# Half of w_out converted in the last part, in two passes over the tokens, with a new order of the attention

## The chip, the cores and the metric

The kernel runs on one core of one Trainium2 chip. What counts is the device time of one execution in microseconds; of several runs the median is taken. The engines have short names: PE multiplies matrices (PEld is its loading of weights), DVE, ACT and POOL work on elements, SP issues most of the transfers (DMA). Each engine works through its own instructions in the order in which they were written, and waits on semaphores for the others. The granted clock of PE is in the profile's rows; 1.00 stands for 2.4 GHz.

## What is computed

Three stages follow each other. First an attention for 4 batches of 8 heads, in which the 1152 queries are averaged in pairs, to 576. Its output, as 2304 tokens of 512 numbers, goes through a soft mixture of 8 experts with 4 slots each. The result goes through a feed-forward layer of width 2048 with `h * cos(h)`:

```python
q_pool = q.reshape(B, H, S // factor, factor, D).mean(axis=3)
scores = scale * np.matmul(q_pool, k.transpose(0, 1, 3, 2))
scores = scores - np.max(scores, axis=-1, keepdims=True)
attn = np.exp(scores)
attn = attn / (np.sum(attn, axis=-1, keepdims=True) + 1e-09)
out = np.matmul(attn, v)
...
logits = x @ phi
d = softmax over tokens; slot_input = d.T @ x
slot_out[e] = np.maximum(slot_input[e] @ w1[e], 0.0) @ w2[e]
x = softmax over slots(logits) @ slot_out
...
h = x @ w_in
g = h * np.cos(h)
y = (g @ w_out).astype(np.float32)
```

Heads are worked on in 16 pairs `p`; the 288 queries of one half `a` of a pair make a half-pair, 32 in all, each with 9 tiles `t` of 128 keys. That gives 288 score tiles.

## The kernel before

**Attention.** For one score tile PE makes the scores of two heads (L460, with the negated maximum added at L463), ACT the exponentials (E, L471), PE the product with V (L498). The row sums of the exponentials (ES, L486 and L488) are added by DVE or by POOL; the table `VEC` names for each half-pair the tiles that DVE adds. The maxima come from an extra product (L415) that DVE reduces (L424). PSUM has four places of two banks for all these; an operation that takes one waits until the last reader of the one before is done. The table `ORDER` lists 2500 operations in the order in which they are written to the engines' queues; nothing else decides it.

**Conversions in the attention.** The weights w_in and w_out are 64-bit numbers; each of 32 tiles of 128 x 512 is turned into 32-bit ones and written to DRAM (`w32`): a load `raw` (512 KB), two ACT steps (L289, L294), three DVE steps (L298, L304, L310), an addition on POOL (L316), a store of 256 KB. Tiles 0 to 15 are w_in, 16 to 31 w_out. There is one buffer `raw` and one `cvt`, so the tiles follow each other, about one per nine score tiles.

**The experts** run from about 500 to 541 us, with their weights streaming in, and end with the slot outputs `soT` (L1280).

**The last part.** `make_p`, `make_p1` and `put_p` multiply `soT` with w_in into `Pst`, which has four tiles of 512 columns. Then the 9 blocks of 256 tokens are worked on in units; a unit is a block and two (at the start one) of the 16 tiles `f` of 128 hidden columns. Per unit PE makes `u` (L1397), ACT and DVE make `g` (L1402 to L1413), DVE splits off a rounded part `hi` (L1415), POOL the rest `lo` (L1417), and PE adds 12 products to two sums `o0` and `o1` (L1433, L1435), each in one of two buffers. For that each tile of w_out is split into `w_hi` and `w_lo` as well (`split_w`, L1317 to L1321; the table `SPLIT` gives the engines). After a block's last unit ACT empties both sums into `ob` (L1445) and SP stores them. `START` lists the first steps by hand (`s` a split, `p` a part of Pst, `u`, `g` and `o` a unit's three steps); after that a loop writes, for unit `no`, `u` of unit no + 4, `g` of unit no + 2 and `o` of unit no, in this order. Before, there are 9 units in the first block and 8 in each of the other eight, 73 in all.

## Time and profile before

| | |
|---|---|
| median of 3 runs | 773.59 us (773.06 to 776.13) |
| the profiled execution | 778.18 us |
| its span in the profile | 776.4 us |
| PE, DVE, ACT, POOL busy in the span | 737.1, 587.7, 448.9, 409.5 us |
| moved by DMA | 101.48 MB, 131 GB/s on average |

The profiled execution took 4.59 us more than the median of the runs, and 1.78 us of it lie around the span. Sums are made against its own time. PE's records overlap, since one matmul is fed in while the one before drains; so "busy" says when PE had something in flight, and a dense run is read from the distance of the starts. Idle time is told with what ended it, the releaser.

### The profile page before, as it was taken

The page shows a single profiled execution, that of the slowest core. Times are in us where ns is not written, and L with a number is a line of the kernel's source. Part 1 is how long each engine was busy: PE and PEld are TensorE (multiplying, and loading weights), DVE is VectorE, ACT ScalarE, POOL GpSimd, SP SyncE. Part 2 cuts the span into 40 slices and gives each one's busy share as a digit, 9 for nine tenths or more (in the row PEclk, how much of TensorE's full clock was granted, in tenths as well). Part 3 has the DMA queues.
Part 4 walks back from the last instruction along what each step waited for, and adds up shares of the span by engine and source line. Part 5 has one row for each costly group of instructions (what it writes and reads, how often), then busy time and mean ns, then how long its engine had stood idle before and what let it go on. Part 6 is the DMA issues. An engine that isn't in the chain of part 4 may idle for free.

```text
span 776.4 us, 16372 instructions
## 1 busy us (share of the span) xinstructions
PE 737.1 (95%) x6336; PEld 532.1 (69%) x6336; DVE 587.7 (76%) x935; ACT 448.9 (58%) x838; POOL 409.5 (53%) x340
## 2 busy tenths in 40 slices
PE   5999999999899999999989998899999999999997
PEld 3766667676676676677666766433678888888886
DVE  6899999988888889899889897322686656565652
ACT  2556656576565666566566653223767666656661
POOL 1476666775669574856456630013765444444442
PEclk9999999999999999999999999999999999999999
DMA  8444465366654654646153456599801010000101
GB/s 201 111 122 142 116 194 143 100 164 174 198 144 137 199 137 140 185 138 162 52 157 103 140 164 211 190 365 385 302 1 28 27 29 28 10 17 28 29 28 27
DMA packets 86482, 101.48 MB, mean 131 GB/s; under 512 B 48260, under 2 KB 48260, under 8 KB 86404
## 3 DMA queue, kind: packets, MB, share of 16 engines
q1 hardware_dynamic: 80384, 100.09, 43.1%
q10 hardware_dynamic: 6020, 0.34, 0.6%
q8 instruction: 50, 0.82, 0.4%
q14 instruction: 28, 0.23, 0.1%
HBM read 87.10 MB, written 13.11 MB: 129 GB/s over the span
## 4 chain that ended last, share of the span: by engine, by line
PE 48%; DVE 9%; ACT 2%; issue 2%; POOL 1%; ACTq 0%; DVEq 0%; POOLq 0%
PE o L1433 16%; PE o L1435 8%; PE mx L498 6%; PE mx L460 4%; DVE nm L424 2%; PE po L1262 2%; PE u L1397 2%; PE h L1229 2%; PE mx L415 2%; DVE ES L488 1%; PE mx L463 1%; PE pm L1341 1%; POOL ES L488 1%; ACT E L471 1%; PE mx L442 0%
## 5 line engine op out<-in xcount | busy, mean ns | idle before, releaser
L488 POOL TENSOR_TENSOR ES<-ES,E 128x576 f32<-128x576 f32 x142 | 208.2, 1467 | 94.5 <-DVE ES L488 66.6
L424 DVE TENSOR_REDUCE nm<-mx 128x2 f32<-128x768 f32 x240 | 221.3, 950 | 26.7 <-PE mx L415 25.8
L471 ACT ACTIVATE E<-mx 128x576 f32<-128x576 f32 x288 | 177.4, 651 | 83.3 <-PE mx L463 62.6
L460 PE MATMUL mx<-Q,kX 64*128 64x288 f32 x1152 | 171.5, 314 | 9.9 <-DVE nm L424 4.7
L498 PE MATMUL mx<-E,vn 128*64 128x288 f32 x1152 | 157.7, 414 | 3.0 <-DVE nm L424 2.2
L1417 POOL TENSOR_TENSOR lo<-g,hi 128x512 fp32r<-128x512 f32 (+1 forms) x73 | 94.3, 1291 | 110.4 <-DVE hi L1415 106.1
L460 PEld LDWEIGHTS mx<-Q,kX 64*128 64x128 f32 x1152 | 111.8, 190 | 30.3 <-DVE nm L424 11.5
L498 PEld LDWEIGHTS mx<-E,vn 128*64 128x64 f32 x1152 | 75.8, 137 | 59.1 <-ACT E L471 8.0
L1433 PE MATMUL o<-w_hi,hi 128*128 128x512 f32 x288 | 113.1, 393 | 0.7 <-DVE hi L1415 0.7
L1435 PE MATMUL o<-w_lo,hi 128*128 128x512 f32 x288 | 113.2, 393 | 0.3 <-DVE w_lo L1321 0.3
L415 PE MATMUL mx<-kX,Q 64*128 64x384 f32 x480 | 87.6, 387 | 5.7 <-DVE nm L424 4.7
L460 PE MATMUL mx<-Q,kY 64*128 64x288 f32 x576 | 87.2, 297 | 0.0
L463 PE MATMUL mx<-NM,one_row 64*128 64x288 f32 x576 | 86.9, 296 | 0.0
L1433 PE MATMUL o<-w_hi,lo 128*128 128x512 f32 x288 | 77.4, 389 | 0.0
L1404 DVE SCALAR_TENSOR_TENSOR r<-t,u 128x512 f32<-128x512 f32 (+1 forms) x73 | 49.4, 679 | 36.4 <-ACT t L1402 35.8
L1402 ACT ACTIVATE t<-u 128x512 f32<-128x512 f32 (+1 forms) x73 | 43.0, 591 | 58.0 <-PE u L1397 57.9
L1413 DVE SCALAR_TENSOR_TENSOR g<-r,u 128x512 f32<-128x512 f32 (+1 forms) x73 | 49.6, 679 | 35.5 <-ACT r L1411 34.8
L316 POOL TENSOR_TENSOR cvt<-cvt 128x512 uint32<-128x512 uint32 x32 | 43.4, 1357 | 61.9 <-DVE cvt L310 28.7
L415 PEld LDWEIGHTS mx<-kX,Q 64*128 64x128 f32 x480 | 44.9, 190 | 28.6 <-DVE nm L424 10.9
L488 DVE TENSOR_TENSOR ES<-ES,E 128x576 f32<-128x576 f32 x81 | 61.5, 759 | 2.8 <-POOL ES L488 0.5
L1433 PEld LDWEIGHTS o<-w_hi,lo 128*128 128x128 f32 x288 | 54.1, 188 | 11.5
L1433 PEld LDWEIGHTS o<-w_hi,hi 128*128 128x128 f32 x288 | 54.2, 188 | 10.8 <-DVE hi L1415 0.9
(227 smaller groups left out, 1016.2 us busy)
## 6 DMA issues: line engine op xcount, KB each, us to landing
w<-in_moe_w_dram SPq DMA_DIRECT2D x85, 256.0 KB
...
```

The costliest lines, as they stand in the source:

```text
L415: nc.tensor.matmul(out=m[:, h, 0:384], lhsT=Q1[p % 2][hs, AT[i]:AT[i] + 128], rhs=X[p][hs, ks], start=True, stop=True)
L424: nc.vector.tensor_reduce(out=nm3[p][:, i, :, c:c + 1], in_=m[:, :, 0:384], axis=AX.X, op=ALU.max)
L460: nc.tensor.matmul(out=sc[:, h, 0:HF], lhsT=x[hs, ks], rhs=y[hs, qs], start=(n == 0), stop=False)
L463: nc.tensor.matmul(out=sc[:, h, 0:HF], lhsT=one_row[hs, :], rhs=NM[p % 2][hs, qs], start=False, stop=True)
L471: nc.scalar.activation(out=e, in_=sc[:, :, 0:HF], func=AF.Exp, scale=1.0 / 16.0)
L488: eng.tensor_tensor(out=ES[p, a], in0=ES[p, a], in1=E[p, a, t], op=ALU.add)
L498: nc.tensor.matmul(out=av_t[p, a, g][64 * h:64 * h + 64, 0:HF], lhsT=vn[p][:, h, t, :], rhs=E[p, a, t][:, h, :], start=(t == g), stop=(t = ...
L1404: nc.vector.scalar_tensor_tensor(out=r, in0=t, scalar=MAGIC, in1=u, op0=ALU.subtract, op1=ALU.subtract)
L1413: nc.vector.scalar_tensor_tensor(out=g, in0=r, scalar=1.0, in1=u, op0=ALU.subtract, op1=ALU.mult)
L1417: nc.gpsimd.tensor_tensor(out=lo[:, 0:n], in0=g, in1=hi[:, 0:n].bitcast(FP32), op=ALU.subtract)
L1433: nc.tensor.matmul(out=o, lhsT=x, rhs=w_hi[ff], start=(ff == 0 and not part), stop=bool(part and ff == NF - 1))
L1435: nc.tensor.matmul(out=o, lhsT=x, rhs=w_lo[ff], start=False, stop=False)
```

## The change

`NU` falls from 32 to 24: tiles 24 to 31, the second half of w_out, are no longer converted in the attention. `ORDER` has 2436 operations, in a new order throughout, and `VEC` is new. The last part goes over the tokens twice. In the first pass (units 0 to 36) the first eight tiles `f` are used, and each block's sums are stored to DRAM (`part_o`); in the second pass (units 37 to 72) the other eight, and DVE adds the sums that are loaded back (`kept`). The eight conversions run in the first pass, as `THEN` says: for each tile a load four units ahead (for the first in unit 5), ACT's steps in unit t, DVE's first two in t + 1, sign and POOL's addition in t + 2, the split in t + 4, with t = 7, 11, ... 35. The tile isn't written to DRAM and read back; the split takes it from `cvt`. `raw` and `cvt` take over the buffers of `win1`. Two rounds of `put_p` move from `START` to units 9 and 11.

```diff
 GAHEAD = 2
-FIRST = (1, 1, 2, 2, 2, 2, 2, 2, 2)
-SPLIT = (0, 1, 1, 3, 1, 1, 1, 3, 2, 0, 1, 0, 3, 3, 0, 1)
+FIRST = (1, 1, 2, 2, 2)
+SPLIT = (0, 1, 1, 3, 1, 1, 1, 3, 1, 1, 1, 1, 1, 1, 1, 1)
...
     ("g", 0), ("s", 3), ("g", 1), ("p", 1, 0, 512), ("u", 2), ("o", 0), ("s", 5), ("s", 6), ("s", 4), ("u", 3),
-    ("g", 2), ("u", 4), ("o", 1), ("g", 3), ("p",), ("g", 4), ("s", 7), ("o", 2), ("p", 2), ("s", 11), ("u", 5),
-    ("u", 6), ("s", 9), ("s", 10), ("p", 3), ("s", 14), ("g", 5), ("o", 3), ("s", 8), ("s", 15), ("o", 4),
-    ("g", 6), ("s", 13), ("s", 12), ("u", 7), ("g", 7), ("u", 8), ("u", 9), ("o", 5), ("g", 8), ("u", 10),
-    ("g", 9), ("o", 6), ("u", 11), ("g", 10), ("o", 7), ("o", 8), ("o", 9),
+    ("g", 2), ("u", 4), ("o", 1), ("g", 3), ("s", 7), ("p",), ("u", 5), ("g", 4), ("o", 2), ("u", 6), ("g", 5), ("u", 7),
+    ("o", 3), ("g", 6), ("u", 8), ("g", 7), ("o", 4), ("u", 9),
 )
+def then():
+    do = {9: [("p", 2)], 11: [("p", 3)]}
+    for f in range(8, 16):
+        t = 4 * (f - 8) + 7
+        for step, at in enumerate((max(t - 4, 5), t, t + 1, t + 2, t + 4)):
+            do.setdefault(at, []).append(("c", f, step))
+    return do
+THEN = then()
...
 VEC = (
-    "468", "1", "45", "2468", "25", "237", "4", "1267",
-    "36", "6", "6", "12367", "68", "67", "15", "7",
-    "568", "1", "4578", "126", "4", "24568", "4", "2367",
-    "234", "17", "238", "137", "67", "123568", "2345678", "1234567",
+    "58", "12", "7", "125", "128", "14", "25", "13568",
+    "23", "68", "123", "7", "56", "56", "48", "1346",
+    "168", "12", "4567", "26", "125", "28", "478", "2",
+    "348", "1", "127", "6", "678", "368", "2345678", "1234567",
 )
 ORDER = (
-    "020304050709060G080H0A0OXsXt0PXu0Q0R0M0N0E0F0C0D0S0I0J0K0L2429010T2A0U0X0Y0V0b0W0m23250B2C0n0p0t0x0qXvXwXxXyXz26"
...
+    "0v470X0i0Y27282BXx0o0s0-X+000Z100f0g0w0z0a0+12130dXy0e14150b0c1819111C1D0j4A161G1H1A1E2W2Q2X171B0k0l1FXz2RX-1J1K"
...
     NU_I = HP * DFF // 512
-    NU = NU_I + NF
+    NU = NU_I + NF // 2
     w32 = [dr.tile([128, 512], FP32, name=f"w32_{i}") for i in range(NU)]
     cv = {}
+    cv_p = [lambda shape, tag: per.tile(shape, U32, tag=tag, name=tag)]
     def conv_load(i):
-        if i >= NU:
-            return
         if i < NU_I:
...
             src = w_out[(i - NU_I) * 128:(i - NU_I + 1) * 128, :]
-        raw = per.tile([128, 512, 2], U32, tag="raw", name="raw")
+        raw = cv_p[0]([128, 512, 2], "raw")
         nc.sync.dma_start(out=raw.rearrange("p a b -> p (a b)"), in_=src)
...
         raw = cv[i]
-        t = per.tile([128, 2, 512], U32, tag="cvt", name="cvt")
+        t = cv_p[0]([128, 2, 512], "cvt")
         t, r = t[:, 0], t[:, 1]
...
         TB = 256
+        NA = NF // 2
+        cv_p[0] = lambda shape, tag: wo.tile(shape, U32, tag="win1_0" if tag == "raw" else "win1_1", name=tag)
+        part_o = [dr.tile([128, DM], FP32, name=f"po{i}") for i in range(NTOK // 128)]
         Pst = [op.tile([128, 512], F32R, bufs=1, name=f"Pst{f}") for f in range(DFF // 512)]
-        win1 = [wo.tile([128, 2, 512], FP32, name=f"win1_{kk}") for kk in range(HP)]
+        win1 = [wo.tile([128, 2, 512], FP32, tag=f"win1_{kk}", name="win1") for kk in range(HP)]
         spread = op.tile([128, 4, 192], F32R, bufs=1, name="spread")
...
+        def late_w(f, step):
+            i = NU_I + f
+            if step == 0:
+                conv_load(i)
+            elif step == 1:
+                conv_act(i)
+                conv_low(i)
+            elif step == 2:
+                conv_clamp(i)
+                conv_shift(i)
+            elif step == 3:
+                conv_sign(i)
+                conv_round(i)
+            else:
+                w_lo[f] = wo.tile([128, DM], F32R, tag=f"w_lo{f}", name="w_lo")
+                split_w(f, cv.pop(i).bitcast(FP32))
         def load_w(f):
...
-        def split_w(f):
+        def split_w(f, w=None):
+            w = w_lo[f].bitcast(FP32) if w is None else w
             if SPLIT[f] // 2:
-                nc.vector.tensor_copy(out=w_hi[f], in_=w_lo[f].bitcast(FP32))
+                nc.vector.tensor_copy(out=w_hi[f], in_=w)
             else:
-                nc.scalar.activation(out=w_hi[f], in_=w_lo[f].bitcast(FP32), func=AF.Copy)
+                nc.scalar.activation(out=w_hi[f], in_=w, func=AF.Copy)
             eng = nc.gpsimd if SPLIT[f] % 2 else nc.vector
-            eng.tensor_tensor(
-                out=w_lo[f], in0=w_lo[f].bitcast(FP32), in1=w_hi[f].bitcast(FP32), op=ALU.subtract
-            )
+            eng.tensor_tensor(out=w_lo[f], in0=w, in1=w_hi[f].bitcast(FP32), op=ALU.subtract)
...
         units = []
-        for blk in range(NTOK // TB):
-            f0 = 0
-            for n in FIRST if blk == 0 else (UF,) * (NF // UF):
-                units.append((blk, f0, n))
-                f0 += n
+        for half in range(2):
+            for blk in range(NTOK // TB):
+                f0 = half * NA
+                for n in FIRST if blk == 0 and half == 0 else (UF,) * (NA // UF):
+                    units.append((blk, f0, n))
+                    f0 += n
         us, gs = {}, {}
...
-        acc = {}
+        acc, kept = {}, {}
...
             last = i == len(units) - 1
+            second = f0 >= NA
+            first_f, last_f = (NA, NF - 1) if second else (0, NA - 1)
+            if second and f0 == NA:
+                kept[blk] = wo.tile([128, 2, DM], FP32, tag=f"win1_{2 + blk % 2}", name="kept")
+                for s in range(2):
+                    nc.sync.dma_start(out=kept[blk][:, s], in_=part_o[2 * blk + s])
...
                 ff = f0 + f
-                if ff == 0 and part == 0:
+                if ff == first_f and part == 0:
                     acc[blk, s] = ps_o.tile([128, DM], FP32, tag=f"o{s}", name=f"o{s}")
...
                 x = (lo if part else hi)[:, f, s * 128:(s + 1) * 128]
-                nc.tensor.matmul(out=o, lhsT=x, rhs=w_hi[ff], start=(ff == 0 and not part), stop=bool(part and ff == NF - 1))
+                nc.tensor.matmul(out=o, lhsT=x, rhs=w_hi[ff], start=(ff == first_f and not part), stop=bool(part and ff == last_f))
                 if not part:
...
                 ob = op.tile([128, DM], FP32, tag="ob", name="ob")
-                if last:
-                    h = DM // 2
-                    nc.scalar.activation(out=ob[:, 0:h], in_=o[:, 0:h], func=AF.Copy, scale=-TWOPI)
-                    nc.vector.tensor_scalar(out=ob[:, h:], in0=o[:, h:], scalar1=-TWOPI, scalar2=None, op0=ALU.mult)
-                else:
+                if not second:
                     nc.scalar.activation(out=ob, in_=o, func=AF.Copy, scale=-TWOPI)
+                    nc.sync.dma_start(out=part_o[2 * blk + s], in_=ob)
+                    return
+                nc.vector.scalar_tensor_tensor(out=ob, in0=o, scalar=-TWOPI, in1=kept[blk][:, s], op0=ALU.mult, op1=ALU.add)
...
                     store(x[0])
-            if f0 + n == NF and not last:
+            if f0 + n == last_f + 1 and not last:
                 for s in range(2):
...
                 make_p(*a, pm)
-                if a[2] == 512:
-                    for i in range(4):
-                        load_w(NF - 8 + 4 * a[0] + i)
...
                 ng += 1
+            for f, *args in THEN.get(no, ()):
+                {"p": more_p, "c": late_w}[f](*args)
             emit_o(no)
...
```

The tables alone don't show what moves. Three places follow, with line numbers of before and after, each as the engine's instructions stand there in a row.

DVE late in the attention, around the maxima of the last pair of heads (nm), before:

```order
L513 TENSOR_TENSOR avs<-mx,avs 128x288
L424 TENSOR_REDUCE nm_6630<-mx 128x2
L298 TENSOR_SCALAR cvt<-cvt 128x512
L304 TENSOR_SCALAR cvt<-cvt 128x512
L486 TENSOR_TENSOR ES<-E 128x576
L488 TENSOR_TENSOR ES<-ES,E 128x576 x2
L310 SCALAR_TENSOR_TENSOR cvt<-raw,cvt 128x512
L424 TENSOR_REDUCE nm_6630<-mx 128x2 x3
L488 TENSOR_TENSOR ES<-ES,E 128x576 x2
```

and after:

```order
L519 TENSOR_TENSOR avs<-mx,avs 128x288
L430 TENSOR_REDUCE nm_6591<-mx 128x2
L494 TENSOR_TENSOR ES<-ES,E 128x576
L430 TENSOR_REDUCE nm_6591<-mx 128x2 x2
L494 TENSOR_TENSOR ES<-ES,E 128x576
L430 TENSOR_REDUCE nm_6591<-mx 128x2 x3
L494 TENSOR_TENSOR ES<-ES,E 128x576
L430 TENSOR_REDUCE nm_6591<-mx 128x2
L595 TENSOR_TENSOR xT<-avs,mx 128x576
```

The three conversion steps (cvt) are gone, and the sums (ES) stand singly between the maxima.

DVE at the start of the last part, from the cast of `w_hi` of tile 7 on, before:

```order
L1317 CAST w_hi_7937<-w_lo 128x512
L1321 TENSOR_TENSOR w_lo<-w_lo,w_hi_7941 128x512
L1404 SCALAR_TENSOR_TENSOR r<-t,u 128x512 x2
L1321 TENSOR_TENSOR w_lo<-w_lo,w_hi_7939 128x512
L1372 CAST Pst_7915<-pm 128x512
L1321 TENSOR_TENSOR w_lo<-w_lo,w_hi_7944 128x512
L1413 SCALAR_TENSOR_TENSOR g<-r,u 128x512
L1415 CAST hi<-g 128x512
L1317 CAST w_hi_7938<-w_lo 128x512
L1321 TENSOR_TENSOR w_lo<-w_lo,w_hi_7938 128x512
```

and after:

```order
L1345 CAST w_hi_7867<-w_lo 128x512
L1387 SCALAR_TENSOR_TENSOR p_lo<-pm,p_hi 128x256
L1431 SCALAR_TENSOR_TENSOR r<-t,u 128x512
L1440 SCALAR_TENSOR_TENSOR g<-r,u 128x512
L1442 CAST hi<-g 128x512
L1431 SCALAR_TENSOR_TENSOR r<-t,u 128x512
L1440 SCALAR_TENSOR_TENSOR g<-r,u 128x512
L1442 CAST hi<-g 128x512
L1431 SCALAR_TENSOR_TENSOR r<-t,u 128x512
L1440 SCALAR_TENSOR_TENSOR g<-r,u 128x512
```

The splits of the later tiles and the copy of Pst (L1372) are gone from between the steps of the units; r, g and hi follow each other.

POOL at the end of the first pass; w_hi_7874 and w_hi_7875 are tiles 14 and 15. Before, behind the splits of the start, it had nothing but `lo` (L1417 x66). After:

```order
L322 TENSOR_TENSOR cvt<-cvt 128x512
L1444 TENSOR_TENSOR lo<-g,hi 128x512 x2
L1349 TENSOR_TENSOR w_lo<-cvt,w_hi_7874 128x512
L1444 TENSOR_TENSOR lo<-g,hi 128x512 x2
L322 TENSOR_TENSOR cvt<-cvt 128x512
L1444 TENSOR_TENSOR lo<-g,hi 128x512 x2
L1349 TENSOR_TENSOR w_lo<-cvt,w_hi_7875 128x512
L1444 TENSOR_TENSOR lo<-g,hi 128x512 x31
```

and PE, where unit 40 begins to use both, after:

```order
L1424 MATMUL u<-cT_7634,Pst_7845 128x256 x2
L1466 MATMUL o_9214<-w_hi_7874,hi 128x512
L1468 MATMUL o_9214<-w_lo,hi 128x512
L1466 MATMUL o_9217<-w_hi_7874,hi 128x512
L1468 MATMUL o_9217<-w_lo,hi 128x512
L1466 MATMUL o_9214<-w_hi_7875,hi 128x512
L1468 MATMUL o_9214<-w_lo,hi 128x512
L1466 MATMUL o_9217<-w_hi_7875,hi 128x512
L1468 MATMUL o_9217<-w_lo,hi 128x512
```

The split of tile 15 comes behind the `lo` of unit 41, and the sixth product of unit 40 reads its w_lo.

## Rows read from the trace of the kernel before

**Rows 1.** The page's busy line: us, share of the span, instructions.
```profile
PE 737.1 (95%) x6336; PEld 532.1 (69%) x6336; DVE 587.7 (76%) x935; ACT 448.9 (58%) x838; POOL 409.5 (53%) x340
```

**Rows 2.** Stretches: from:to, length; busy PE, PEld, DVE, ACT, POOL; clock, DMA, GB/s.
```profile
20.00:350.00 330.00, 318.69 (x3441) 228.86 (x3443) 297.92 (x427) 205.40 (x380) 221.03 (x161) 0.99 0.54 150
350.00:480.00 130.00, 122.35 (x1313) 87.34 (x1313) 112.94 (x173) 77.39 (x145) 66.38 (x51) 0.99 0.45 132
```

**Rows 3.** Timeline of PE, attention: start, us, instructions.
```profile
321.68 0.29 PE L460 MATMUL mx<-Q,kX 64*128 64x288 f32 x2
...
322.21 0.51 PE L415 MATMUL mx<-kX,Q 64*128 64x384 f32 x4
322.65 1.68 PE L498 MATMUL mx<-E,vn 128*64 128x288 f32 x12
324.26 0.62 PE L415 MATMUL mx<-kX,Q 64*128 64x384 f32 x4
```

**Rows 4.** Groups, 350 to 480 us: count, busy, mean ns, idle before.
```profile
L488 POOL TENSOR_TENSOR ES<-ES,E 128x576 f32<-128x576 f32 x33 | 48.5, 1471 | 26.3 <-DVE ES L488 19.0 <-ACT E L471 6.0 <-DVE kY L401 0.2
...
L498 PE MATMUL mx<-E,vn 128*64 128x288 f32 x324 | 43.8, 413 | 0.1
...
L488 DVE TENSOR_TENSOR ES<-ES,E 128x576 f32<-128x576 f32 x29 | 22.0, 759 | 1.7 <-POOL ES L488 0.5 <-ACT E L471 0.2
...
L415 PE MATMUL mx<-kX,Q 64*128 64x384 f32 x116 | 19.8, 371 | 0.6 <-DVE nm L424 0.6
```

**Rows 5.** Chain of waits, 350 to 480 us: shares of the stretch by line.
```profile
by line: PE mx L498 24.0%; PE mx L460 15.8%; DVE nm L424 10.5%; PE mx L415 6.6%; DVE ES L488 6.3%; PE mx L463 4.7%; issue 4.4%; POOL ES L488 3.3%; ACT E L471 2.6%; DVE cvt L304 1.9%; PE mx L442 1.5%; DVE cvt L310 1.5%; DVE avs L513 1.2%; DV
```

**Rows 6.** Stretch of the last part, as rows 2.
```profile
640.00:700.00 60.00, 60.00 (x283) 50.08 (x283) 36.26 (x61) 37.39 (x65) 26.42 (x21) 1.00 0.07 18
```

**Rows 7.** Timeline of one unit of the last part, four engines.
```profile
701.04 0.40 PE L1397 MATMUL u<-cT,Pst 128*128 128x256 f32 x2
...
704.03 0.40 PE L1397 MATMUL u<-cT,Pst 128*128 128x256 f32 x2
704.26 0.39 PE L1433 MATMUL o<-w_hi,hi 128*128 128x512 f32 x1
...
701.01 1.09 ACT L1445 ACTIVATE ob<-o 128x512 f32<-128x512 f32 x2 [0.74 <-PE o L1433]
...
705.61 0.63 ACT L1411 ACTIVATE r<-r 128x512 f32<-128x512 f32 x1
...
704.59 0.43 DVE L1415 CAST hi<-g 128x512 fp32r<-128x512 f32 x1
...
706.35 0.69 DVE L1413 SCALAR_TENSOR_TENSOR g<-r,u 128x512 f32<-128x512 f32 x1 [0.56 <-ACT r L1411]
...
705.19 1.30 POOL L1417 TENSOR_TENSOR lo<-g,hi 128x512 fp32r<-128x512 f32 x1 [2.19 <-DVE hi L1415]
```

**Rows 8.** Conversions (tile cvt), 350 to 480 us: busy DVE, ACT, POOL.
```profile
350.00:480.00 130.00, 13.91 (x24) 10.65 (x16) 10.21 (x8) 0.99 0.45 132
```

**Rows 9.** Timeline of PE, start of the last part: gaps in brackets.
```profile
561.19 0.74 PE L1397 MATMUL u<-cT,Pst 128*128 128x256 f32 x4 [0.69 <-ACT Pst L1374]
...
569.11 0.50 PE L1435 MATMUL o<-w_lo,hi 128*128 128x512 f32 x1 [0.29 <-DVE w_lo L1321]
...
575.13 0.47 PE L1397 MATMUL u<-cT,Pst 128*128 128x256 f32 x2 [0.23 <-DVE g L1413]
...
578.77 0.47 PE L1433 MATMUL o<-w_hi,hi 128*128 128x512 f32 x1 [0.25 <-DVE hi L1415]
```

**Rows 10.** Two lines' instructions: count, ns as min/median/max, first and last start.
```profile
L304 DVE TENSOR_SCALAR cvt<-cvt x8: 417/426/1534, 357.6 to 458.3; 128x512 uint32<-128x512 uint32 x8
...
L1321 POOL TENSOR_TENSOR w_lo<-w_lo,w_hi x11: 1277/1303/1837, 544.0 to 573.4; 128x512 fp32r<-128x512 f32 x11
```

**Rows 11.** Timeline of ACT: two pairs of exponentials.
```profile
350.09 1.19 ACT L471 ACTIVATE E<-mx 128x576 f32<-128x576 f32 x2
...
480.29 1.19 ACT L471 ACTIVATE E<-mx 128x576 f32<-128x576 f32 x2 [0.32 <-PE mx L463]
```

More of the change, by code (lines that the diff above doesn't have):

```diff
@@ new lines @@
+    "2m36374SYC31383C2i393G4T4Y3D352n1z1+1-6E3H2o2p3K4Z3A4K3P3S3L4L4f3B4g3F3JYD3EYF3QYH3I3N3M3O3T4W3W4X3a203e8Z3j3X3b"
+    "YI3f3UYJ4M3Y4U4V4N3R3V3Z3dYG3k3h4a3i4b3n3o21YK3r3v3c4Q223s4p3g3l3p3m3qYM3w4qYLYN4R4c3u3y3z4l4n4d4e6F6G4u4m4x4o6J"
+    "6CYP4-534v4yYQ503t3x544zYRYO51574j4k6H6I6K494w4+5256YU585A5BYS4h4i6L5C5G5K6M6N5D6S55YT595E5H5I5L4r6T8c5O5P6c6d3+"
+    "3-4sYVYWYX5F5J405N5R6n4t5T5W5S6o5U5a5e5M8aYY5QatYZ5X5b5Y5c5f5i5j6O6P5V5Z4142436Y6e6U446Z6f5d5h5l5g6D5mYa6Q6V6R5n"
+    "5rYcYb5kau5v6Wav5o5p5s5w6X5z5+6a6b6g8f8g6l5q5u8d6m8i8e8h6hYd5y5t5x606i61458j468kAd8l6y6-73Yf6z5-70Yg7177746j787B"
@@ new lines @@
+    "6k7C62Yh63758q6p6q8m8n6+72Ye8r64Yk767AYiYj7E7F6r797D6saw7G7H8y7K8z7O7S7L7PYl7I657TYm6t8u6u6vYn7J7N7R7V6w8v6x7W90"
+    "918s7X7a7Y7M8t7b7Q7U7e7iax667fYoYp7j8+Ae7m7r7v8-7c7n678oYsYq8p7Z7dYr687h7l8b7w7pAg7g7k7s7q8w7z8x927+957o9681827t"
+    "YtYuYvAhAiay93947x7u7y8084AlCh9Baz859K9N9C9LYw9O7-9R9S9783989V9Z9P9W696A86AjAna+9a9T8788YxYy999AAk9M9Q9UAoAp9X9Y"
+    "9c9d9eAm9f9bAy9gAz9i9j9m9q9n898A9D9E9r9F8B8C9hAf9l9p9t9G9HYz9I9JY+9k9oa-9uAuAvb0Y-Aw9v9y9w9zAxA0A4A+A19sCiA5A8B2"
+    "9x9-A3Z1Z2Z3Z6Z0Z4Ck9+A2A7B3A9ABA-ACAsAtADAE8DAH8EAIB0ALB1AMZ5BDElBEAPA6AQAqArB4AA8FClCmB5B6AFB78GZ78ICpb1Z9ZAb2"
@@ new lines @@
+    "b3B88HAGAKAJAOASZ8BOBHATBRANBPBSBIBVBWZBBZ8JBa8KBTCnCoARBdBiBjZEBXBQBUCqBYBBBbBeBCCrBFBcBgCsBGBfBhAUCtAV8LZC8P8M"
+    "BkZD8QBJBKBmBnBqBuBoBrD2EoB9BABLBlBpBtD3BvBxByAWZF8TBM8UBN8N8OD48RBzBsBwC0ZH8SD5B+C4C1ZIC5CyZJC2C8CzCCZGZKb4D8CD"
+    "D9C9ZM8V8W8XCwC+ZLAX8YD0D1AYB-CjC-C6C3C7AZCBCFAaCuCGCxCvZNCHHACID6CLEmCPZPCMD7DAZQCQCACECTCUDFZODGCJZREpb5DBDCCK"
+    "COCSCWCNCREqEtDSCVDVZUCXZSDTDNDWDXDODZDdDhDaDbDJHDDeDiAbCYAcCZCaDKDfErDHEsDUDYDIZTDcZVEuEvDLEwDMDgZXDkDlDmDDExDn"
+    "DqDuDyDrDjDEDvZYDoZZFAE+DsDwDpDtDxZcZWDzDPZaDQFBDRE-D-E1E0E2F0F1E4E8D+E5E6EyE9EzECEDCbCcCdF2F3EGEHFHFIE3E7FCF4FD"
@@ new lines @@
+    "F6F7CeZbEBb6EFEJEKEAF8F5ELF9ZdEMZfFEHBEEEIEPETEQEUENZgFLEXHEEYJEHFERFMHIFFEVZhEOFGESEWEaEbFPFQZeZiEnEZb7FWFXCfFZ"
+    "CgFaFRFSFdFeFhFiFJFKFlZkFmFbFNFOZjEcEdHGFTJHFfFjHKHLHMFYFcFgFkFoEeHHHJZlZnZmFqFpFrHbFuFyG0FvHNFnZoFsHcZpb8b9FwFz"
+    "HREfHOG1HSFtFxF-G3FUHZZqHXFVG5EgG4HaG6bAHYG8GCG9F+G2EhGDGGGHGKGLZsHdGPGAGEHVHeEiHWG7GBGFZrGIZtZvGQGMGJGNGOHTHUGT"
+    "GUHPHQZwGXGbGYGcHkHfZxJIHgGRGVZuZyGZHlHhJJJMGSGWGaGeHsGfHtHxHyHmH+HnH-JFI2I3GdI6I7HoIAIBEjI0GgJKHpEkHCLIGhbBHqHr"
+    "HiGiHzJLI1HjHuJNZzZ+Z-a1bCa0bDbEI5I9IDIEHvHwI4I8ICJOa2JPJQIFIGIJINa3IKIOLJJdIRISJeIWIZIXJZJRGjIHGkILJSJaIIIMGlIa"
@@ new lines @@
+    "IQIUIVJhJiIPa6GmITIdIeIbIhIiIlImJbJXIYIcIga4LLa5IkIoIfJcIjInIpJYIqIrJTJUIsIuIvIwGnGoNMIybFJfIzJ0JGJgbGI+JVJWJjLM"
+    "GpLOJ1LNJ2LQa7a9Jwa8ItIxI-J3GqGsLPbHGrH1LRJxH2J4JkJlaAaBGvGwJoGxGyJ-K2K6JpJsaCK0K3K7aEKAH3JtKBJuJvJ5J6J7JqJrKEKJ"
+    "JmKFK4LSJnK8KCLTLUK1K5K9KDKKaDaFH4KHKIJyJzJ+GzKGG+NPaHaIaJJ8KLKNKRKOKSH5KPKVG-KWKaH0KdaGbILfLgKMLKKeKQaMKbKUKYGt"
+    "KTbJKZLjGuLkKhaKKiLZaLLaKlLlKmLmH6H8KXH7aNH9KpJ9KqKfKjJAaPLVLWLXLYKcKgKkKnKoJBaOKsNNKtaQaRLdLhLeKuKyKvPnLiKzL0L1"
+    "LbbKLcLnL4LqL5aUaSLrKrKwK+L2NSNTNQLoLpKxNRK-L3L7NVNUL8LuLvaTaVbLaXaWM3M6M4aYL6MAMEM7M8aZMIMBMCMFMGaaMJLyJCbMMKM5"
@@ new lines @@
+    "UrUkTfTjUoUsUTUvUwUURpRqTmW3TnUVUXUiUmUqUWW4UYUdW6UuUyUzUlUpUtUeUfWKU+ToV2V6WLU-V3UxV0V7WGWHVFVGVIVJV4V-VAVKWAWB"
+    "W7W8W9TpV1V8V5V9VBVDVETqTrWEWFVCVMVNVQVUVRWVWCWWWDVHVLTsVPVVVOVSVZVaWQVWWRWOWPVTVXVYWIWJVdVhVlVbVeVfViWMTtWNTuVc"
+    "VgWSbUVmbbVjVnVkVoVpWTWUVqVrVsWZWabcWkWlWnWoWrWsWdWeWvWwWzW+WbWcWpX2WfWXWYWmWqX3VtVuWuVvVwWgWhWyX0bVWiWjbWWtWxX6"
+    "X7W-XAXBXEX1XFXJX4X8X5X9XDXHXIVxVyXKbhXMXNbmXQXRXUbeXCXYXGXObXbkXLXPbZbYbqboXSXVXWXTXXXZblXbXcXdXhXlXeXqXibiXmbr"
+    "bsXrbuXgbvbtbdXaXfXjb+b-c0XkXoXnXpbwbxbyc1bjc2bpbnbzc3bf"
```

57 lines of the change are left out of this document (13 added, 44 removed).

## The prediction, made before the changed kernel ran

> **What bounds the kernel now.** I read the page's busy line first, then two stretches of the attention by engine, the chain of waits, and the timeline of the last part. The busy line gives PE 95% and DVE 76% of the span [rows 1], but a share over the whole span says little here, since the program has three stages with different limits. In the attention (20 to 480 us) PE and DVE run side by side: from 20 to 350 us PE is shown busy 318.69 of 330 us and DVE 297.92; from 350 to 480 us PE 122.35 of 130 and DVE 112.94, ACT 77.39, POOL 66.38 [rows 2]. Neither is at its end. Matmuls overlap, so a PE record lasts longer than its turn: a score tile of eight matmuls takes its turn from 321.68 to 322.21, 0.53 us; four matmuls of the maximum 0.44; three products with V (twelve records) from 322.65 to 324.26, 0.54 each [rows 3]. The stretch has 324 records of the product with V, 81 products, as many score tiles, and 116 matmuls of the maximum [rows 4]: 81 x 0.53 + 81 x 0.54 + 29 x 0.44 = 99 us, with transposes and sums on top. So PE waits more than the 7.65 us that are shown. The chain of waits of that stretch has both: PE's lines lead, DVE's maxima have 10.5%, its sums of exponentials (ES) 6.3%, and two of the three DVE steps of a conversion 1.9% and 1.5% [rows 5].
>
> From about 580 us on PE is full: 60.00 of 60 us, with DVE at 36.26, ACT 37.39, POOL 26.42 [rows 6]. One unit takes 704.03 - 701.04 = 2.99 us [rows 7]. There only PE's own work and its waits count.
>
> **The change, part by part.** *The last eight conversions leave the attention.* In the order they are the ones between score tiles 213 and 274 of 288, and the trace has just eight in the stretch 350 to 480: 24 DVE instructions of 13.91 us, 16 of ACT with 10.65, 8 of POOL with 10.21 [rows 8]. They all go. In the same stretch the table VEC leaves 29 instead of 37 of the sums on DVE; eight at a mean of 0.759 are 6.1 us less for DVE, and eight at 1.471 are 11.8 more for POOL [rows 4]. DVE falls from 112.9 to about 93 of 130, POOL goes to 66.4 - 10.2 + 11.8 = 68, ACT to 67. PE's work is the same, matmul for matmul. What that gives is not 20 us, since most of DVE's work there runs beside PE's. The chain tells what stood on the path: 3.4% of 130 us for the two conversion steps that it names, 4.4 us; and of the sums' 6.3%, 8.2 us, eight of 37, 1.8 us [rows 5]. Together 6.2 us. The PE idle time shown, 7.65, is close [rows 2]. The ends are 0 (another DVE or PE instruction takes each place) and the 13.9 us that the conversions take of DVE; with those PE would have 116 us for 99 us plus the rest of its work, so it would hardly wait at all. I take 6.2, nearest to the chain's row.
>
> This is where the trace has PE at 94% and DVE at 87% of the stretch, with weight loads (PEld) at 87.34 of 130, 67% [rows 2]. The Trainium skill (Perfetto Trace Analysis, Identifying the Most-Contended Engine) says that matmul busy share is a bad measure, that the share of weight loads and for Vector the occupancy are fair ones, and that the engine with the highest is the one to relieve. By that DVE is the most contended and the relief would pay nearly in full, the first rival's result below; the chain's row, where PE's lines lead, speaks for less.
>
> *The first 23 half-pairs, up to 350 us,* keep their 24 conversions at nearly the same score tiles; DVE gets 57 instead of 54 sums, 2.3 us more of 298. All of it stands in a new order. I take 0 for this, with the third rival for its price.
>
> *The start of the last part.* The splits of the second half's eight weight tiles are gone there: four subtractions and three casts of DVE, five casts of ACT, four subtractions of POOL; and two rounds of put_p are put off to units 9 and 11. PE's gaps that hang on these are 0.69 (ACT's copy of Pst), 0.29 (a split on DVE), 0.23 and 0.25 (g and hi late behind splits) [rows 9], 1.5 us in all. What could be late next is `win1`, whose last load is issued just before; it stays as it is. I take -1.5, between 0 and -2.5.
>
> *Two passes.* 73 units as before, the same matmuls, so PE's sum stays. Each block has two ends instead of one. ACT empties 18 sums in the first pass and DVE 18 in the second, where ACT emptied 16 before. Per four units (11.96 us) DVE has now 36.26/60 x 11.96 = 7.2; with a late conversion (13.91/8) 9.0, and in the second pass with two emptyings at the 0.69 of another reading from PSUM [rows 7] 8.6. ACT: 7.5, plus half a pair of emptyings 0.55, 1.33 and a cast 0.6, 10.0. POOL: 5.3 + 1.28 + 1.30 = 7.9 [rows 6, 8, 10]. None fills 11.96. The work stands in lumps, so what hides it is the lead of two units: g starts at 706.35 and takes 0.69, hi 0.43 more, 707.5, and PE wants it two units after 704.26, at 710.2 [rows 7]; the spare is near 3 us. In unit 4k + 7 ACT has 1.9 us more and in the next its emptyings, 1.1, together 6.4 of 5.98 us; 0.5 us late, covered.
>
> SP's queue: the load of the next tile's raw words waits for the sign step of the tile before, two units on, and behind it stands the store of a block's sums to DRAM. Its buffer is wanted four units later, so the wait costs nothing; if that cover were gone, PE would wait for about two units, 6 us, per block. 18 stores and 18 loads of 256 KB meet DMA at 0.07 [rows 6].
>
> *The last tile is late.* Tile 15 is cast and split just before unit 39, and unit 40 needs it. On the clock of unit 704.03: sin and square end at 706.24, the cast of w_hi at 706.8; g runs from 706.35 to 707.0, hi follows, lo runs from 707.7 to 709.0 (by the 0.60 from hi to lo at 704.59 and 705.19, and the 1.30 of the row); then POOL's subtraction of 1.30, to 710.3 [rows 7, 10]. PE starts unit 40 at 707.25 and reaches w_lo of tile 15 as its sixth matmul, 5 x 0.23 later, at 708.4. It waits 1.9 us, once, and nothing gives that back. The ends are 0 and 3 (the subtraction took up to 1.837).
>
> *Accumulators.* put_p takes one of two buffers of o1 in units 9 and 11; if they take turns, units 9 and 13 start on the buffer whose emptying has just begun. At a block's end ACT empties from 701.01 to 702.1 while PE's next unit began at 701.28 [rows 7] and wants o1 after two matmuls, at 701.74: 0.4 us in unit 13, nothing in unit 9, where put_p fills the time. The last store is one DVE instruction for ACT's and DVE's halves; I take 0.
>
> **Sum:** -6.2 - 1.5 + 1.9 + 0.4 = -5.4 us. The profiled run of before took 778.18 (span 776.4), so the changed one would take 772.8; against the median of 773.59 that is 768.2. I say 768.0.
>
> **Rivals.** *DVE sets the pace of that stretch,* and the conversions pay in full, 13.9 for 6.2: 760.3. For it: DVE's lines have a good fifth of the chain, and DVE is 87% busy there. Against: PE leads the chain.
> *PE's chain closes up,* nothing is gained in the attention: 774.2. For it: 94% busy; the tail of the attention has few other pairs' maxima to fill in.
> *The new order costs time before 350 us* (the other side). There DVE is 90% busy with no work taken away, and PE idles 330 - 318.69 = 11.3 us [rows 2]. An order that places a few buffers worse could double that: 768 + 11.3 = 779.3. It makes the kernel slower, by the bound, from 9.5 us on. Against it: per half-pair, DVE's and PE's loads are much as before.
> *The late tiles hold up the last part.* The second DVE step of a conversion took 417 at least, 426 in the middle and 1534 ns at most [rows 10]. The Trainium skill (GPSIMD Engine Reference, Specifications) says that GpSimd shares its SBUF interfaces with VectorE and contends with some of its instructions; the 1534 agrees with that, though no row shows the cause. Two such steps and POOL's lumps would eat 2.2 us of the 3 us of spare; another 2 would make PE wait 1 us for each of eight tiles: 776.
>
> **Chances.** Forecast 0.50 (its own range 764 to 771.5), DVE's pace 0.15, PE's chain 0.17, the worse order 0.13, late tiles 0.05. Half a per cent, 3.9 us, is what can be told from no change: 769.7 and 777.5 are the bounds. Faster: the rival at 760 and four fifths of the forecast, 0.55; slower: the worse order and part of the late tiles, 0.16; the rest 0.29. The range reaches from 759 (DVE's pace) to 777 (PE's chain, late tiles) and leaves out the worse order.
>
> **What would show it.** The exponentials that open the 24th half-pair, the pair at 350.09, should stay within 3 us; the attention's last pair, at 480.29, should come about 6 us earlier [rows 11]. In the stretch between, DVE is busy near 93 us. The start of the last part has no PE gap on a split, and PE waits once, on w_lo, some 2 us in the fourth unit of the second pass; otherwise a unit stays at 2.99. I am wrong if the units of the first pass are longer than that, if the first 330 us move by more than a few us, or if DVE's relief turns into idle time of DVE alone.

## The result, and the profile after

The changed kernel takes 762.64 us (median of four runs, 761.58 to 764.05); the kernel before, run beside it, 774.5 (773.06 to 776.13). The ratio is 0.985, with an interval of 0.982 to 0.988. The profiled execution has a span of 761.7 us, where it had 776.4. The profiled one of before is a long one, 778.18 us against the median of 774.5, so of the 14.7 us between the spans about 3 are its own; the medians differ by 11.9.

That is close to the 768 forecast, and says nearly nothing for the reasons behind it. The page's busy line and the stretches of after, chosen to answer to [rows 1, 2, 6]:

```profile
PE 730.1 (96%) x6336; PEld 531.8 (70%) x6336; DVE 588.3 (77%) x939; ACT 446.3 (59%) x841; POOL 415.5 (55%) x349
```

```profile
20.00:330.00 310.00, 309.51 (x3447) 227.62 (x3449) 291.03 (x429) 205.01 (x381) 214.37 (x160) 1.00 0.57 158
330.00:447.00 117.00, 117.00 (x1312) 85.20 (x1310) 95.32 (x145) 66.53 (x129) 63.05 (x49) 1.00 0.35 101
560.00:640.00 80.00, 70.36 (x291) 55.30 (x292) 54.06 (x80) 49.32 (x89) 43.32 (x33) 0.94 0.25 72
670.00:730.00 60.00, 60.00 (x283) 50.09 (x282) 41.94 (x71) 35.33 (x62) 26.34 (x21) 1.00 0.30 88
```

The first two are the attention: the matmuls that took 330 us, up to the start of the 24th half-pair, now take 310, and the last 130 are now 117. PE is idle for 0.5 us in the first and not at all in the second. The third lies in the first pass of the last part, where PE is now idle for 9.6 of 80 us and its clock is granted at 0.94; the fourth is the second pass, full again as before.

Two marks divide the span: the last exponentials of the attention, and the first product that makes `soT`, at the start of the last part. First before's (the pair at 480.29 is [rows 11]), then after's, from the timelines of ACT and PE:

```profile
540.92 0.38 PE L1276 MATMUL t<-gsel,so 128*128 128x128 f32 x1
```

```profile
445.40 2.33 ACT L477 ACTIVATE E<-mx 128x576 f32<-128x576 f32 x4 [0.31 <-DVE rec L562]
...
502.42 0.38 PE L1282 MATMUL t<-gsel,so 128*128 128x128 f32 x1 [0.21 <-ACT so L1278]
```

| | before, us | after, us | change |
|---|---|---|---|
| up to the end of the last exponentials | 481.5 | 447.7 | -33.8 |
| from there to the first product for `soT` | 59.4 | 54.7 | -4.7 |
| last part | 235.5 | 259.3 | +23.8 |
| span | 776.4 | 761.7 | -14.7 |

So of a gain of 38.5 us, six times the 6.2 that was forecast in these places, 23.8 were lost again in the last part, where the forecast came to +0.8. What waits there, in after, from 560 to 660 us (engine, line waited for: us, times, longest):

```profile
...
DVE r L1431 <- ACT t L1429: 26.7, 6, 4.5
ACT cvt L295 <- POOL w_lo L1349: 24.2, 6, 4.1
PEld u L1424 <- issue: 13.6, 7, 2.6
PE u L1424 <- DVE g L1440: 10.9, 6, 2.2
...
PE o L1468 <- POOL w_lo L1349: 3.1, 1, 3.1
```

ACT's first instruction of a conversion, line 295, waits six times for some 4 us each, for POOL's subtraction `w_lo` of the tile before. The timeline shows one of these and what hangs on it (rows of POOL, ACT, DVE and PE):

```profile
608.73 0.62 ACT L1347 ACTIVATE w_hi<-cvt 128x512 fp32r<-128x512 f32 x1
609.06 1.29 POOL L1444 TENSOR_TENSOR lo<-g,hi 128x512 fp32r<-128x512 f32 x1 [0.44 <-DVE hi L1442]
...
610.78 1.29 POOL L1444 TENSOR_TENSOR lo<-g,hi 128x512 fp32r<-128x512 f32 x1 [0.43 <-DMA po<-ob]
612.03 1.29 POOL L1349 TENSOR_TENSOR w_lo<-cvt,w_hi 128x512 fp32r<-128x512 f32 x1
613.35 0.67 ACT L295 ACTIVATE cvt<-raw 128x512 f32<-128x512 f32 x1 [4.00 <-POOL w_lo L1349]
613.92 0.65 ACT L300 ACTIVATE cvt<-raw 128x512 uint32<-128x512 uint32 x1
614.47 0.58 ACT L1429 ACTIVATE t<-u 128x512 f32<-128x512 f32 x1
615.08 0.69 DVE L1431 SCALAR_TENSOR_TENSOR r<-t,u 128x512 f32<-128x512 f32 x1 [4.45 <-ACT t L1429]
...
617.17 0.47 PE L1424 MATMUL u<-cT_r,Pst 128*128 128x256 f32 x2 [1.42 <-DVE g L1440]
...
627.32 1.29 POOL L1349 TENSOR_TENSOR w_lo<-cvt,w_hi 128x512 fp32r<-128x512 f32 x1
```

`cvt`, the words under conversion, is one buffer. Tile f+1 wants it in the unit in which tile f is split, and POOL's subtraction is the last reader. The subtraction itself comes late: `w_hi` is there at 609.35, but in POOL's queue the `lo` of two units (609.06 and 610.78) stand ahead of it. ACT stands still for 4.00 us until it ends; `t`, which the next unit needs, is queued behind; DVE stands still for 4.45, `g` comes late, and PE 1.42 us. From one subtraction to the next are 15.3 us, where four units take 11.96. So a tile costs PE 3.3 us on average. The idle time shown is only part of that: the three units after this wait take 3.42, 3.23 and 3.29 us from `u` to `u`, where 2.99 is the dense pace.

### The profile page after: what moved, and what is told of

It is laid out like the page before. It is cut to its first block, busy times and chain, and to the rows that moved or that the text cites. A ratio compares the mean times of both kernels' runs of the same rounds, so it can differ in the third digit from the quotient of the medians.

```text
span 761.7 us, 16413 instructions
## 1 busy us (share of the span) xinstructions
PE 730.1 (96%) x6336; PEld 531.8 (70%) x6336; DVE 588.3 (77%) x939; ACT 446.3 (59%) x841; POOL 415.5 (55%) x349
## 4 chain that ended last, share of the span: by engine, by line
PE 80%; DVE 11%; ACT 3%; POOL 3%; DMA 1%; issue 1%; SPq 0%; DVEq 0%; POOLq 0%
PE mx L504 20%; PE mx L466 16%; PE o L1466 10%; PE mx L421 7%; PE o L1468 5%; PE mx L469 5%; DVE hi L1442 2%; DVE g L1440 2%; PE po L1268 2%; PE h L1235 2%; DVE nm L430 2%; PE mx L448 2%; DVE r L1431 1%; PE mx L388 1%; PE u L1424 1%; POOL lo L1444 1%
## 5 line engine op out<-in xcount | busy, mean ns | idle before, releaser
L494 POOL TENSOR_TENSOR ES<-ES,E 128x576 f32<-128x576 f32 x150 | 215.6, 1437 | 81.3 <-DVE ES L494 49.9
L477 ACT ACTIVATE E<-mx 128x576 f32<-128x576 f32 x288 | 174.5, 652 | 59.9 <-PE mx L469 44.0
L466 PE MATMUL mx<-Q,kX 64*128 64x288 f32 x1152 | 165.1, 304 | 0.1
L1444 POOL TENSOR_TENSOR lo<-g,hi 128x512 fp32r<-128x512 f32 (+1 forms) x73 | 96.6, 1323 | 121.3 <-DVE hi L1442 110.8
L1468 PE MATMUL o<-w_lo,hi 128*128 128x512 f32 x288 | 115.8, 402 | 3.1 <-POOL w_lo L1349 3.1
L1466 PE MATMUL o<-w_hi,hi 128*128 128x512 f32 x288 | 117.8, 409 | 0.2
L421 PE MATMUL mx<-kX,Q 64*128 64x384 f32 x480 | 84.1, 380 | 1.8 <-DVE nm L430 1.3
L1468 PEld LDWEIGHTS o<-w_lo,hi 128*128 128x128 f32 x288 | 56.2, 195 | 13.5 <-POOL w_lo L1349 3.5
L1466 PEld LDWEIGHTS o<-w_hi,hi 128*128 128x128 f32 x288 | 56.0, 194 | 12.3 <-DVE hi L1442 1.2
L1466 PEld LDWEIGHTS o<-w_hi,lo 128*128 128x128 f32 x288 | 54.7, 190 | 11.9
```

What stands on the lines that cost most here:

```text
L421: nc.tensor.matmul(out=m[:, h, 0:384], lhsT=Q1[p % 2][hs, AT[i]:AT[i] + 128], rhs=X[p][hs, ks], start=True, stop=True)
L466: nc.tensor.matmul(out=sc[:, h, 0:HF], lhsT=x[hs, ks], rhs=y[hs, qs], start=(n == 0), stop=False)
L477: nc.scalar.activation(out=e, in_=sc[:, :, 0:HF], func=AF.Exp, scale=1.0 / 16.0)
L494: eng.tensor_tensor(out=ES[p, a], in0=ES[p, a], in1=E[p, a, t], op=ALU.add)
L1444: nc.gpsimd.tensor_tensor(out=lo[:, 0:n], in0=g, in1=hi[:, 0:n].bitcast(FP32), op=ALU.subtract)
L1466: nc.tensor.matmul(out=o, lhsT=x, rhs=w_hi[ff], start=(ff == first_f and not part), stop=bool(part and ff == last_f))
```

## Experiments

**Is it the one buffer?** Two kernels change only that place. The first gives `cvt` two spaces, both free by then:

```diff
-        cv_p[0] = lambda shape, tag: wo.tile(shape, U32, tag="win1_0" if tag == "raw" else "win1_1", name=tag)
+        cvt_tags = ["win1_2", "win1_1"] * NA
+        def cv_tile(shape, tag):
+            return wo.tile(shape, U32, tag="win1_0" if tag == "raw" else cvt_tags.pop(0), name=tag)
+        cv_p[0] = cv_tile
```

> Changed kernel with two buffers instead of one for the words under conversion (cvt takes the space of win1_2 and win1_1 in turn); the work and its order are the same. Theory A (the one buffer): ACT's first step on tile f+1 has to wait until POOL has subtracted tile f, and holds back the t, sin and square queued behind it; so the period of four units in the first pass falls from 15.3 to 12 to 12.5 us, seven or eight times 3 us, 20 to 24 us in all: about 740 us. Rival B (the lumps of work themselves, contention between POOL and DVE, or the sums in DRAM): the period stays at 15 us or above 14, and the time at 757 us or more.

It took 743.47 us (742.17 to 744.49), 0.959 of before (0.956 to 0.961), 19.2 us less than the changed kernel. The line's summary gives six subtractions, with their first and last start, in the changed kernel and then with two buffers:

```profile
L1349 POOL TENSOR_TENSOR w_lo<-cvt,w_hi x6: 1287/1290/1446, 581.4 to 657.9; 128x512 fp32r<-128x512 f32 x6
```

```profile
L1354 POOL TENSOR_TENSOR w_lo<-cvt,w_hi x6: 1295/1300/1447, 575.4 to 637.6; 128x512 fp32r<-128x512 f32 x6
```

Five periods took 76.5 us and now take 62.2: 15.3 and 12.4 us each. Theory A holds: the period is in its range and far from the rival's 14. The gain of 19.2 us is just under its 20 to 24. The last part is down to 240.3 us.

The second keeps one buffer and issues the split a unit earlier:

```diff
-        for step, at in enumerate((max(t - 4, 5), t, t + 1, t + 2, t + 4)):
+        for step, at in enumerate((max(t - 4, 5), t, t + 1, t + 2, t + 3)):
```

> Changed kernel, one buffer as it was, but the split of a late tile (cast on ACT, subtraction on POOL) is issued one unit earlier, three units after the tile's first step instead of four. Theory A (the one buffer): the subtraction is over up to one unit, 2.99 us, before ACT wants the buffer, so that most of the 3.3 us per four units goes: 742 to 750 us. Rival B (lumps, contention, sums in DRAM): the same work in the same lumps, within 4 us of the changed kernel, or slower, since the split now stands right behind the rounding step.

747.27 us (747.11 to 747.83), ratio 0.964 (0.961 to 0.966); the period is 13.6 us. The time is in theory A's range; the period gave back half of the 3.3 us, not most. With the same buffers, the same work and an earlier release, 15.4 us of the loss are gone. Lumps, contention or DRAM traffic by themselves can't give this.

**Do two passes cost anything?** Here the late tiles are not converted; converted words of the first eight are loaded and split in their place.

> Changed kernel without the conversions in the last part: the last eight tiles of w_out are not converted; in their place the converted words of the first eight are loaded from DRAM, into two buffers in turn, and split at the same units, so that the result is that of other weights. What is left is two passes, the sums in DRAM and the late splits. Theory A (the one buffer holds up ACT; two passes themselves cost nothing): last part, from the first projection of soT to the end, at 236 to 241 us as against 235.5 in one pass and 240.2 with two buffers, the whole 738 to 743 us. Rival (passes, sums in DRAM or splits cost of themselves): above 245 us, the whole above 747 us.

739.35 us (738.54 to 739.66). The last part is 234.6 us, below theory A's range for it and below the 235.5 of one pass; the whole time is in its range. From 560 to 620 us PE is full:

```profile
560.00:620.00 60.00, 60.00 (x283) 49.98 (x282) 36.12 (x60) 42.72 (x77) 32.52 (x26) 1.00 0.20 67
```

So the second pass, 18 stores and 18 loads of sums and the late splits cost nothing that PE sees, but for the wait on the last tile.

**A better schedule, first try.** Late tiles closer together, two `cvt` buffers as above, still one for the raw words, and ACT's second step (`conv_low`) a unit later:

```diff
-        t = 4 * (f - 8) + 7
+        t = 7 * (f - 8) // 2 + 7
...
+            elif step == 2:
                 conv_low(i)
-            elif step == 2:
```

> Two buffers for the words under conversion, and the late tiles every three and a half units instead of every four, so that the last is split at unit 35 instead of 39; ACT's scaling of the low words goes one unit later than the absolute values. Theory A with the late last tile as the second cost: PE's wait of 3 us on w_lo in unit 40 goes, and some of the rest: 737 to 741 us, 2 to 6 us below the kernel with two buffers alone. Rival (lumps of work): the same work in less time makes the units of the first pass longer, 744 us or more.

It took 751.22 us (750.76 to 751.35), slower than the 743.47 with the old spacing. The forecast fell, and the time is in the rival's range; but the waits from 545 to 640 us give another reason than the rival's:

```profile
ACT cvt L295 <- DMA raw<-in_moe_w_out_dram: 20.3, 6, 5.7
DVE r L1436 <- ACT t L1434: 17.1, 8, 4.4
```

The same ACT instruction now waits for its load, six times, 20.3 us in all. The load has to wait until the sign step of the tile before has read the only `raw` buffer, and then goes the way from DRAM. By this trace it is the same fault one buffer further.

**Second try:** `raw` doubled as well, loads two units earlier, tiles and splits at other units, `conv_low` back in its place:

```diff
-        t = 4 * (f - 8) + 7
-        for step, at in enumerate((max(t - 4, 5), t, t + 1, t + 2, t + 4)):
+        t = (7, 11, 14, 18, 21, 25, 29, 33)[f - 8]
+        for step, at in enumerate((max(t - 6, 5), t, t + 1, t + 2, min(t + 5, 37))):
...
+        cv_tags = {"cvt": ["win1_2", "win1_1"] * NA, "raw": ["win1_3", "win1_0"] * NA}
```

> Kernel two_cvt with a second buffer for the raw words as well, each load two units earlier, the late tiles at units 7, 11, 14, 18, 21, 25, 29, 33 instead of 7, 11, 15 ... 35, and the split five units after a tile's first step (four for the last). Theory A (what is left over the kernel without conversions, 739.4, are ACT's waits for the raw words and for POOL's rounding, and PE's wait for the last tile): 737 to 741 us, 2 to 6 us below two_cvt's 743.5. Rival (lumps of ACT's and DVE's work hold up the units in any case): 743 us or more.

737.45 us (737.21 to 737.89), ratio 0.952 (0.950 to 0.955): the best version, 25.2 us below the changed kernel and 36.6 below before. From 560 to 620 us, with all conversions in place, PE is full:

```profile
560.00:620.00 60.00, 60.00 (x282) 50.01 (x281) 51.23 (x78) 48.40 (x87) 41.58 (x31) 1.00 0.29 94
```

No wait for `cvt`, `raw` or `w_lo` is listed for PE or ACT from 560 to 660 us. DVE at 51.23 of 60 and ACT at 48.40 do not hurt; the rival with the lumps is out. Which of the changes against the first try did how much, one run can't tell.

**The attention: the order, or the eight conversions less?** Two kernels cross them. The first is the changed kernel with ORDER and VEC of before, without the 64 steps of the last eight conversions; the second the kernel before with the new ORDER and VEC and these 64 steps put back behind the same score tiles.

> Changed kernel with the order of the attention of before (ORDER and VEC of before, the 64 steps of the last eight conversions struck out, everything else in its place). Last part as in the changed kernel, about 259 us. Theory O (the new order gives the gain in the first 23 half-pairs): the exponentials of the 24th half-pair start at 348 to 352 us as before, the last exponentials at 467 to 476, and the whole takes 781 to 793 us. Theory R (taking the eight conversions out frees the attention, the order matters little): the last exponentials come at 447 to 457 us and the whole takes 762 to 772 us.

> Kernel of before with the changed kernel's order of the attention and its table VEC, the 64 steps of the last eight conversions put back behind the same score tiles as before; last part in one pass as before, about 236 us. Theory O (the order): the 24th half-pair starts at 328 to 334 us, the last exponentials come at 452 to 462, and the whole takes 747 to 757 us. Theory R (removal of the conversions): the last exponentials come at 470 us or later, and the whole takes 765 to 775 us.

They took 795.54 us (792.92 to 796.98) and 774.66 (773.17 to 776.47). From the traces:

| attention | 24th half-pair starts | from there to the start of the last exponentials |
|---|---|---|
| old order, 32 conversions (before) | 350.6 | 130.2 |
| old order, 24 | 347.8 | 124.7 |
| new order, 32 | 329.9 | 151.8 |
| new order, 24 (changed) | 330.0 | 117.1 |

The first 23 half-pairs go by the two tables alone, 18 to 21 us, with the same conversions in them. In the last nine, taking the eight conversions out of the old order gives 5.5 us in these traces, and the new order another 7.6. The 5.5 are uncertain: the execution traced of before lies 3 us above the median of its kernel, that of the old order with 24 conversions 2.6 below. By the medians this kernel is 20.3 us slower than before (775.21 beside it); its last part is 23.7 us longer and the way there 0.6 shorter, so its whole attention gained some 3 us, where the two traces have 8.3.

The old order's 795.5 us lie 2.5 above theory O's range, its two marks at 347.8 and 473.2 us in or next to it. In the second kernel theory O holds for the first mark, 329.9 us; the last exponentials at 481.7 us and the whole time of 774.66 are theory R's figures. Between the last two rows of the table lie 34.7 us. In the old order the same conversions cost 5.5, so most of it is likely the price of putting them at the old places of a new order; no run here separates the places from the work. The stretches of the second kernel show PE idle for 20.9 us in the second, at least 12.4 of them in waits for ACT's exponentials, and a granted clock of 0.92:

```profile
20.00:330.00 310.00, 309.43 (x3450) 227.28 (x3451) 291.75 (x429) 205.31 (x382) 214.63 (x160) 1.00 0.57 159
330.00:481.00 151.00, 130.07 (x1305) 89.09 (x1302) 112.79 (x168) 74.16 (x143) 73.61 (x57) 0.92 0.39 116
```

**Which of the two tables?** ORDER sets the sequence, VEC which engine takes a sum of exponentials. Each was put back alone.

> Changed kernel with the table VEC of before (which sums of exponentials DVE takes and which POOL) and the new ORDER. Theory S (the gain before 350 us comes of the other division of the sums between DVE and POOL): the 24th half-pair starts at 340 to 352 us instead of 330. Theory W (it comes of the order, that is, of where the work stands in the queues of the engines): it starts at 328 to 336 us, whatever engine takes a sum.

> Changed kernel with ORDER of before (the 64 steps of the last eight conversions struck out) and the new table VEC. Against the run with both tables of before, whose 24th half-pair started at 347.8 us. Theory S (division of the sums): it starts at 330 to 338 us. Theory W (the order): it starts at 344 us or later.

The 24th half-pair started at 367.4 us with the new ORDER and the old VEC (811.4 us in all, one run), and at 387.2 with the old ORDER and the new VEC (833.2, one run); 330.0 and 347.8 when the tables belong together. The first is in neither theory's range. The second is "344 us or later" as theory W had it, but 39 us beyond the 347.8 that W meant. So neither stands: the gain can't be put down to one table; each of these orders reaches the mark 37 to 39 us later with the other's division of the sums. What PE waited for, in the first of the two, 22 to 367 us:

```profile
PE mx L421 <- DVE nm L430: 8.0, 9, 1.4
PE mx L466 <- DVE xT L595: 3.1, 1, 3.1
PE mx L448 <- DVE Z L436: 2.6, 5, 0.7
```

**Is PE at its floor in the new order?** The three DVE steps of the 24 conversions in the attention are left out, once in each order, to see what PE gets back.

```diff
     def conv_clamp(i):
+        if i < NU:
+            return
...
     def conv_shift(i):
+        if i < NU:
+            return
...
     def conv_sign(i):
+        if i < NU:
+            return
```

> Kernel old_order (changed kernel with both tables of before) with the three DVE steps of the 24 conversions in the attention left out, 72 instructions, 24 x 1.74 = 41.7 us of DVE; the weights are then not those of the reference. Theory D (in the old order PE waits for PSUM tiles that DVE empties too late, and the new order takes these waits away; the matmuls themselves take some 309 us of the first 23 half-pairs): the 24th half-pair starts at 330 to 337 us instead of 347.8. Theory P (the waits of the old order lie elsewhere: in the order of PE's own work, on ACT or POOL): 342 us or later.

> Changed kernel (new tables) with the same 72 DVE instructions left out. Theory D: PE has no waits left that DVE could give back, so the 24th half-pair starts within 2 us of 330.0 and the last exponentials come within 2 us of 447.7. If DVE still sets the pace in the new order, the 24th half-pair starts at 322 us or earlier.

The 24th half-pair started at 336.5 instead of 347.8 us in the old order, and at 330.2 instead of 330.0 in the new. The stretch to there, first the old order with its DVE steps, then without them:

```profile
20.00:347.50 327.50, 316.87 (x3445) 226.85 (x3447) 298.12 (x427) 205.44 (x381) 221.89 (x161) 1.00 0.54 150
20.00:336.50 316.50, 313.34 (x3449) 227.40 (x3451) 258.48 (x356) 204.97 (x381) 214.82 (x161) 1.00 0.55 156
```

and the new order without them:

```profile
20.00:330.00 310.00, 309.27 (x3446) 227.25 (x3447) 258.75 (x357) 205.24 (x381) 211.00 (x160) 1.00 0.56 159
```

Both times are in theory D's ranges, by one run of each. In the old order 40 us less of DVE gave 11.3; in the new one 32 us less of DVE gave nothing. So the new order runs this stretch close to PE's own pace, with DVE busy for 94% of the time.

## Why the prediction was right and wrong

That the time lay in the range is luck: two steps failed in opposite directions, by 32 and 23 us. Two of the prediction's own signs of being wrong came: the first 330 us moved by 20, and four units of the first pass took 15.3 us and not 11.96.

**Right in size: the eight conversions, 4.4 of the -6.2.** In the old order they gave 5.5 us by the traces, and by the medians some 3 in the whole attention. The chain of waits [rows 5] had told 4.4 for them; the other 1.8 are sums that VEC moves, which that kernel leaves where they were. So 13.9 us of DVE work [rows 8] were worth two fifths of their length or less; the chain had said a third. The Trainium skill (Perfetto Trace Analysis, Identifying the Most-Contended Engine) has the engine of highest occupancy relieved first; that is DVE, and the prediction read nearly the full price out of it. The runs here go against that price: 5.5 of 13.9 in the last stretch, 11.3 of 40 before it, and nothing in the new order, where DVE at 94% still stands above the weight loads at 73%.

**Wrong: "All of it stands in a new order. I take 0 for this."** This step was off by 20.6 us up to the 24th half-pair, by another 7.6 in the last nine, and by most of the 4.7 in the stretch to the last part (with the old order and 24 conversions that takes 58.8 us, with the new one and 32 conversions 55.0). By the traces that is 32 us. Its rival knew one direction only, and was priced by PE's idle time as shown, 11.3 us. The rows for a better bound were there. I had worked out PE's turns for the last stretch, 99 us, and not for the first: 23 half-pairs have 207 score tiles x 0.53, 207 products x 0.54 and 86 groups of four maximum matmuls x 0.44, 259 us [rows 3]; what else PE does there, transposes and sums, takes 43 us in the trace of after. Together 302 of the 328.6 us from the first exponentials to the 24th half-pair: by that estimate PE was kept from its turns for up to 26 us, more than twice the idle time shown; the rest is in matmul records that last longer. The maximum matmuls show it: from start to next start, 342 of them had 50.4 us of PE in that stretch before, and 348 have 42.4 after. A new order could give back up to 26 us; it gave 20. Nothing ahead of the run told that it would be a good one, but 0 as the value, with a loss as its only alternative, was no fair bound. The first rival's 116 us for the last stretch is what the changed kernel has there, 117.1, though not by the mechanism told: the conversions' leaving was 5.5 of the 13.1 us, or less.

What in the new order removes the waits is only partly told. From the end of a maximum tile's matmuls to the start of DVE's reading it passed 0.69 us on average in the first stretch, now 0.50; in the last 0.79, now 0.34. That DVE empties PSUM sooner agrees with the waits on `nm`, and with the run without DVE's conversion steps. Which places of the order do it stays open.

**Wrong: late conversions covered, 0.** The prediction summed each engine's work per four units and looked at lumps. The sums were right: in the second try, with more buffers, that work is hidden entirely. The step that failed is the list of waits the change adds: it followed the `raw` buffer on SP's queue, and not `cvt`, on ACT's. ACT's first step of the next tile and POOL's subtraction stand in the same unit, four units from the last, and for each of the seven tiles after the first that takes 3.3 us from PE, 23 us in all. A second buffer alone gave 19.2 us back. The rival of the late tiles priced 1 us for each of eight and gave the wrong cause, with a chance of 0.05.

**Start, passes, accumulators: -1.5, 0, +0.4.** In the version without late waits the last part takes 232.7 us, 2.8 less than before; these terms together, forecast at -1.1, so came to -2.8. The put-off put_p and the second set of emptyings show no wait of PE.

**Last tile: +1.9.** The wait came once, in unit 40, as told, but with 3.06 us, just beyond the upper end of its bound. The one buffer is not the reason: with two it is 3.06 us as well. The clock of the prediction let the cast of `w_hi` follow the square at once; in the trace of after the cast waits for POOL's rounding of the tile, and the subtraction takes 1.45 us:

```profile
653.21 1.29 POOL L322 TENSOR_TENSOR cvt<-cvt 128x512 uint32<-128x512 uint32 x1
654.53 0.63 ACT L1347 ACTIVATE w_hi<-cvt 128x512 fp32r<-128x512 f32 x1 [1.07 <-POOL cvt L322]
657.87 1.45 POOL L1349 TENSOR_TENSOR w_lo<-cvt,w_hi 128x512 fp32r<-128x512 f32 x1
```

Without the conversions the wait was 1.7, near the 1.9 of that clock.

**SP's queue: 0.** Right for the changed kernel. The 20.3 us of the first try show what stood behind that cover.
